# Linear attention and a two-branch FFN on one core: v of two batches cast in flight, a PSUM bank per pair, output units in halves, and a new order of work

## The chip, the cores and the metric

The kernel runs on one core of a Trainium2 chip. The metric is the device time of one execution in microseconds (us). Three runs of the kernel before gave 251.06, 251.57 and 251.97; the median is 251.57 us.

## What is computed

Eight batches of eight heads, 576 positions, 64 elements a head, go through linear attention; the result, as 4608 rows of 512, goes through a feed-forward block with two branches that are multiplied:

```python
q_p, k_p = (phi(q), phi(k))          # phi(x) = (x if x > 0 else exp(x) - 1) + 1
kv = np.einsum('bhsd,bhse->bhde', k_p, v)
z = np.sum(k_p, axis=2)
num = np.einsum('bhsd,bhde->bhse', q_p, kv)
den = np.einsum('bhsd,bhd->bhs', q_p, z)[..., None] + 1e-06
attn = num / den
x = attn.transpose(0, 2, 1, 3).reshape(4608, 512)
a = x @ w1                           # 512 x 1024
b = x @ w2
out = (a * b @ w3) @ w_out           # 1024 x 1024, 1024 x 512
```

Inputs and output are float32 in HBM; the kernel multiplies in bf16 and sums in float32.

## The kernel before

**The order is written out.** The body defines small functions ("steps") and a long string `ORDER` (L478 to L548) that lists every step with its arguments. The loop at L555 runs through it; each engine and each DMA queue gets its instructions in that order and runs them in that order, with semaphores between engines. The string is written out in the source, and nothing is moved at run time. In the names below the first number is a batch or chunk, the last letter an engine (`v` VectorE or DVE, `a` ScalarE or ACT) or a queue (`s` SyncE's or SP's, `g` GpSimd's or POOL's). `GATES` (L550) makes a few of SP's loads wait for an earlier load.

**Opening.** Since nothing is applied between w3 and w_out, the kernel multiplies them once: `l3` and `lo` load w3 and w_out by DMAs that cast to bf16, `w3t` transposes a block of w3 on TensorE (PE), `w3c` copies it, `wa` and `wf` multiply, and `wc` copies the product, `wf_sb` (L376 to L413). `lw` loads w1 and w2 with a cast (L144). `warm` steps are matmuls on zeros that keep PE busy (L113).

**Attention of a batch.** Of the 576 positions, 512 are worked on per batch and the remaining 64 of two batches together (names with `r`; they make chunk 8). `ld` loads k, q or v of a batch, 1 MB of float32, into one of five buffers (L119). phi is max(x, 0) + 1 on DVE (`t`, L172), exp on ACT (`x`, L166), and the minimum of the two on DVE (`m`, L180), which in this kernel takes two heads at a time. `v_` casts v to bf16 into the tile `vt` (L217), in which each head has 64 columns of v and one column of ones, so that one product gives kv and z. For batches 0 and 1 `kv` (L230) multiplies pairs of heads, 128x130; `kc` and `kh` (L268, L279) copy the two diagonal blocks into `kvb`. All four pairs share one tile of two PSUM banks. From batch 2 on, `kk` (L254) multiplies head by head in half-width matmuls and `kg` copies. q is transposed by PE for batches 0 and 1 (`qt`, `qc`) and by a transposing DMA on SP from batch 2 on (`qd`, L299). `na` multiplies transposed q with `kvb` for a pair (L311), `nd` divides on DVE: add, reciprocal, multiply (L317 to L319). The quotient is transposed by PE (`xp`, `xc`) for chunks 0 to 2 and by a DMA (`xd`, L363) for 3 to 7. `nar` and `ndr` are the same for the remaining positions.

**Feed-forward of a chunk.** For each of eight blocks of 128 of the 1024 columns, `f` makes a and b in two PSUM buffers with four matmuls each (L420; `fk` does a part of them), `ac` copies a to SBUF on ACT (L434), `ab` multiplies on DVE (L439). `o` makes an output block of 128 rows with eight matmuls (L445), `oc` copies it (L451), `st` stores it (L463) through POOL's queue, in the last chunks through SP's; for chunk 8 a store is two DMAs of 64 rows. `ol` (L465 to L476) is the last output unit: it goes in two halves of the columns, one copied by DVE and stored through SP's queue, one by ACT and through ACT's.

**PSUM.** Eight banks: four one-bank buffers (tag `mm`: warm, w3t, wf, qt, xp, f, o) and two two-bank buffers (tag `at`: wa, kv, kk, na, nar).

Of the kernel before, what the change touches and what calls it, by code (L numbers as in the profile page):

```python
# [18 lines left out]
def kernel(  # L19
# [71 lines left out]


    @step
    def const(i):
        if i == 0:
            nc.vector.memset(zero, 0.0)  # L96
        elif i == 1:
            make_identity(nc, ident)
        elif i == 2:
            for t in vts:  # L100
                nc.vector.memset(t[:, :, :, D:E1], 1.0)
        elif i == 3:
# [13 lines left out]
    @step  # L116
    def ld_(n, b, h0, nh, queue):
        t = got(raw, (n, b), ld, [P, H * W], F32, "ld", f"{n}32")
        return queue_of[queue].dma_start(  # L119
            out=t[:, h0 * W:(h0 + nh) * W].rearrange("p (h x) -> p h x", x=W),  # L120
            in_=src[n][b, h0:h0 + nh, 0:NJ * P, :].rearrange("h (p j) d -> p h (j d)", j=NJ))

# [53 lines left out]
    @step  # L176
    def m(n, b, h0, hp):
        d = got(ph, (n, b), phi_p, [P, KC, NJ, 2, D], BF16, n)
        s = slice((2 * hp - h0) * W, (2 * hp - h0 + 2) * W)
        nc.vector.tensor_tensor(  # L180
            out=d[:, hp].rearrange("p j u d -> p u j d"),
            in0=ts[n, b, h0][:, s].rearrange("p (u j d) -> p u j d", u=2, j=NJ),
            in1=es[n, b, h0][:, s].rearrange("p (u j d) -> p u j d", u=2, j=NJ), op=ALU.min)
# [31 lines left out]
    @step  # L215
    def v_(b, h0, nh, eng):
        copy_of[eng](  # L217
            out=vts[b % len(vts)][:, :, h0:h0 + nh, 0:D],
            in_=raw["v", b].rearrange("p (h j d) -> p j h d", h=H, j=NJ)[:, :, h0:h0 + nh])

    @step
    def vr(b, eng):
        s = b % 2
        r = slice(s * R, (s + 1) * R)
        copy_of[eng](out=vrz[r, s, :, 0:D],
                     in_=raw["vr", b // 2][r].rearrange("p (h d) -> p h d", d=D))
# [3 lines left out]
    def kv(b, hp):  # L230
        o = got(ps, ("kv", b), at_ps, [P, 2, 512], F32, "at", "kvp")
        g, a = divmod(hp, 2)
        kj = ph["k", b]
        kr = ph["kr", b // 2, 2 if b > 1 else b]
        vt = vts[b % len(vts)]
        dst = o[:, g, a * PW:(a + 1) * PW]
        for j in range(NJ):
            nc.tensor.matmul(dst, kj[:, hp, j].rearrange("p u d -> p (u d)"),
                             vt[:, j, 2 * hp:2 * hp + 2, :].rearrange("p h e -> p (h e)"),
                             start=(j == 0), stop=False)  # L240
        nc.tensor.matmul(dst, kr[:, hp * P:(hp + 1) * P],
                         vrz[:, b % 2, 2 * hp:2 * hp + 2, :].rearrange("p h e -> p (h e)"),
                         start=False, stop=True)
# [4 lines left out]
    def kk(b, hp):  # L248
        o = got(ps, ("kk", b), at_ps, [P, 2, 512], F32, "at", "kvp")[:, 0]
        kj, kr, vt = ph["k", b], ph["kr", b // 2, 2], vts[b % len(vts)]  # L250
        for j in range(NJ + 1):
            for u in range(2):
                h = 2 * hp + u
                nc.tensor.matmul(o[u * D:(u + 1) * D, hp * E1:(hp + 1) * E1],  # L254
                                 kj[:, hp, j, u] if j < NJ else kr[:, h * D:(h + 1) * D],
                                 vt[:, j, h] if j < NJ else vrz[:, b % 2, h],
                                 start=(j == 0), stop=(j == NJ))

    @step
# [48 lines left out]
    def na(b, hp):  # L308
        o = ps["na", b, hp] = at_ps.tile([P, 2, 512], F32, tag="at", name="nd")
        for j in range(NJ):  # L310
            nc.tensor.matmul(o[:, j // 2, (j % 2) * 256:(j % 2) * 256 + PW],  # L311
                             sb["qt", b][:, hp, j * P:(j + 1) * P],
                             kvb[b][:, hp].rearrange("p u e -> p (u e)"),
                             start=True, stop=True)

    def divide(o, r, dst):
        nc.vector.tensor_scalar_add(out=r, in0=o[:, :, :, D], scalar1=1e-6)  # L317
        nc.vector.reciprocal(out=r, in_=r)  # L318
        nc.vector.tensor_tensor(  # L319
            out=dst, in0=o[:, :, :, 0:D],  # L320
# [3 lines left out]
    def nd(b, hp):  # L324
        x = got(sb, ("xn", b), att, [P, NJ, DM], BF16, "xn")
        r = small.tile([P, NJ, 2], F32, tag="r4", name="r")
        o = ps["na", b, hp].rearrange("p i (a x) -> p (i a) x", a=2)[:, :, 0:PW]
        divide(o.rearrange("p j (u e) -> p j u e", e=E1), r,
               x[:, :, hp * P:(hp + 1) * P].rearrange("p j (u e) -> p j u e", u=2))

    @step
    def nar(b):
        o = ps["nar", b] = at_ps.tile([P, 2, 512], F32, tag="at", name="ndr")
        for hp in range(KC):
            g, a = divmod(hp, 2)
            nc.tensor.matmul(o[:, g, a * PW:(a + 1) * PW], sb["qtr", b // 2][:, hp, :],  # L336
                             kvb[b][:, hp].rearrange("p u e -> p (u e)"),
# [252 lines left out]
```

## Time and profile before

| what | value |
|---|---|
| median of three runs | 251.57 us |
| profiled execution: time | 251.52 us |
| profiled execution: span of the core | 249.7 us, 4327 instructions |
| PE busy | 236.0 us (95%) |
| DVE busy | 164.1 us (66%) |
| ACT busy | 122.9 us (49%) |
| chain that ended last: PE, DMA | 56%, 32% |
| DMA moved | 50.10 MB, mean 201 GB/s |
| granted TensorE clock | 1.000 |
| f (L420, chunks 0 to 7): a and b | 66.0 us each, 256 matmuls each |
| o (L445) | 62.9 us, 267 matmuls recorded |
| last matmul ends, last store lands, span ends | 246.27, 248.6, 249.7 us |

The time of an execution is some 1.8 us longer than the span between its first and last instruction. Matmuls are pipelined: the 379 ns that the page gives for one of 512 columns holds its latency, and four that follow each other start 0.86 us after the four before them. In lines of the timeline the first number is the start and the second the length in us, and the bracket at the end says how long the engine sat idle before and what ended that. A few matmul records are missing, which can look like a gap of 0.22 us.

### The profile page before, as it was taken

How to read it: one execution, taken by the hardware profiler on the slowest of the kernel's cores; microseconds unless marked ns; L12 is line 12 of the kernel's file. 1: busy time of each engine (PE TensorE's matmuls, PEld its weight loads, DVE VectorE, ACT ScalarE, POOL GpSimd, SP SyncE). 2: the span in 40 equal slices, each digit the busy share in tenths (PEclk: the TensorE clock that was granted, in tenths of full speed). 3: DMA queues.
4: the chain of work that ended last, by engine and by line, in shares of the span. 5: the costliest groups of instructions: out<-in, count | busy, mean ns of one | idle time of the engine just before them, and what ended most of it. 6: DMA issues, size and time to landing. Idle time of an engine off the chain costs nothing.

```text
span 249.7 us, 4327 instructions
## 1 busy us (share of the span) xinstructions
PE 236.0 (95%) x1620; PEld 122.9 (49%) x1636; DVE 164.1 (66%) x364; ACT 122.9 (49%) x190; POOL 36.4 (15%) x59
## 2 busy tenths in 40 slices
PE   6897889979999989999999999999999999999994
PEld 6654844445444555454444454544544444444442
DVE  7518764977868999959649889786775365042320
ACT  3409554776956774665744835153352332323211
POOL 8554720001100210011000032200001100000000
PEclk9999999999999999999999999999999999999999
DMA  6999999999998999999999699975409511210155
GB/s 120 204 265 348 214 198 294 314 248 319 336 240 227 281 294 287 211 248 351 189 265 335 182 248 260 291 175 107 105 12 128 179 22 21 91 38 29 55 144 153
DMA packets 69621, 50.10 MB, mean 201 GB/s; under 512 B 41312, under 2 KB 64096, under 8 KB 69600
## 3 DMA queue, kind: packets, MB, share of 16 engines
q1 hardware_dynamic: 60416, 31.86, 54.1%
q0 software_dynamic: 9040, 17.83, 28.0%
q8 instruction: 13, 0.21, 0.3%
q10 hardware_dynamic: 144, 0.13, 0.2%
q14 instruction: 8, 0.07, 0.1%
HBM read 38.80 MB, written 9.44 MB: 193 GB/s over the span
## 4 chain that ended last, share of the span: by engine, by line
PE 56%; DMA 32%; DVE 4%; issue 3%; ACT 2%; POOL 1%; SPq 0%; ACTq 0%; POOLq 0%; DVEq 0%
PE a_ps L420 17%; PE o_ps L445 17%; PE b_ps L420 17%; DMA v<-in_v_dram 13%; DMA q<-in_q_dram 9%; DMA w_sb<-in_moe_w_dram 4%; DMA wo<-in_moe_w_out_dram 3%; DMA k<-in_k_dram 3%; DVE xn L319 2%; PE nd L311 2%; PE kvp L254 1%; POOL w3b L159 1%; PE ndr L336 1%; PE o_ps L472 1%; ACT vt L217 1%
## 5 line engine op out<-in xcount | busy, mean ns | idle before, releaser
L420 PEld LDWEIGHTS <-w_sb 128*128 128x128 bf16 x576 | 55.6, 98 | 64.6 <-issue 0.6
L439 DVE TENSOR_TENSOR ab<-a_sb,b_ps 128x512 bf16<-128x512 f32 x72 | 49.0, 684 | 43.7 <-PE b_ps L420 40.1
L434 ACT COPY a_sb<-a_ps 128x512 f32<-128x512 f32 x72 | 42.1, 584 | 58.8 <-PE a_ps L420 52.7
L420 PE MATMUL a_ps<-xt,w_sb 128*128 128x512 bf16 x256 | 66.0, 379 | 0.5 <-ACT xt L358 0.5
L420 PE MATMUL b_ps<-xt,w_sb 128*128 128x512 bf16 x256 | 66.0, 379 | 0.0
L445 PE MATMUL o_ps<-wf_sb,ab 128*128 128x512 bf16 x267 | 62.9, 379 | 1.0 <-issue 0.2
L445 PEld LDWEIGHTS <-ab 128*128 128x128 bf16 x280 | 26.4, 98 | 30.3 <-DVE ab L439 1.2
L463 POOL DMA_DIRECT2D out_dram<-o_sb x24 | 14.5, 605 | 148.7 <-ACT o_sb L451 130.9
L451 ACT COPY o_sb<-o_ps 128x512 f32<-128x512 f32 x24 | 14.0, 585 | 34.1 <-PE o_ps L445 31.9
L319 DVE TENSOR_TENSOR xn<-nd,r 128x512 bf16<-128x512 f32 x32 | 22.1, 692 | 1.1
L166 ACT ACTIVATE e<-q 128x1024 bf16<-128x1024 f32 x16 | 16.5, 1056 | 1.8 <-DMA q<-in_q_dram 1.8
L166 ACT ACTIVATE e<-k 128x1024 bf16<-128x1024 f32 x16 | 16.4, 1058 | 0.9 <-DMA k<-in_k_dram 0.8
L451 DVE COPY o_sb<-o_ps 128x512 f32<-128x512 f32 x11 | 7.6, 687 | 8.0 <-PE o_ps L445 8.0
L217 ACT CAST vt<-v 128x1024 bf16<-128x1024 f32 (+1 forms) x11 | 10.2, 933 | 5.4 <-PE kvp L254 2.7
L180 DVE TENSOR_TENSOR k<-t,e 128x512 bf16<-128x512 bf16 x32 | 12.2, 418 | 0.4 <-ACT e L166 0.2
L172 DVE TENSOR_SCALAR t<-q 128x1024 bf16<-128x1024 f32 x16 | 10.9, 688 | 2.1 <-DMA q<-in_q_dram 2.1
L180 DVE TENSOR_TENSOR q<-t,e 128x512 bf16<-128x512 bf16 x32 | 11.9, 420 | 0.2
L311 PE MATMUL nd<-kvb,qt 128*128 128x130 bf16 x128 | 10.9, 220 | 0.9 <-DVE kvb L268 0.4
L172 DVE TENSOR_SCALAR t<-k 128x1024 bf16<-128x1024 f32 x16 | 10.5, 688 | 1.2 <-DMA k<-in_k_dram 1.1
L311 PEld LDWEIGHTS <-qt 128*128 128x128 bf16 x128 | 8.7, 98 | 4.9 <-DVE xn L319 1.0
L113 PE MATMUL warm<-zero 128*128 128x128 bf16 x116 | 9.2, 241 | 1.2 <-DVE zero L96 1.2
L318 DVE RECIPROCAL r<-r 128x8 f32<-128x8 f32 (+1 forms) x40 | 8.1, 202 | 1.4
(76 smaller groups left out, 191.6 us busy)
## 6 DMA issues: line engine op xcount, KB each, us to landing
v<-in_v_dram SPq DMA_DIRECT2D x6, 1024.0 KB, 9.8
k<-in_k_dram SPq DMA_DIRECT2D x6, 1024.0 KB, 8.7
q<-in_q_dram SPq DMA_DIRECT2D x6, 1024.0 KB, 9.2
out_dram<-o_sb POOLq DMA_DIRECT2D x24, 256.0 KB, 6.1
w3b<-in_moe_w_dram POOLq DMA_DIRECT2D x8, 256.0 KB, 8.1
out_dram<-o_sb SPq DMA_DIRECT2D x7, 256.0 KB, 2.3
v<-in_v_dram POOLq DMA_DIRECT2D x3, 512.0 KB, 18.9
out_dram<-o_sb SPq DMA_DIRECT2D x9, 128.0 KB, 2.4
```

Of the source, the lines that this page charges most:

```text
L166: return nc.scalar.activation(out=e[:, 0:nh * W], in_=raw[n, b][:, h0 * W:(h0 + nh) * W], func=AF.Exp)
L172: nc.vector.tensor_scalar(out=d[:, 0:nh * W], in0=raw[n, b][:, h0 * W:(h0 + nh) * W], scalar1=0.0, scalar2=1.0, op0=ALU.max, op1=ALU.add)
L180: nc.vector.tensor_tensor(out=d[:, hp].rearrange("p j u d -> p u j d"), in0=ts[n, b, h0][:, s].rearrange("p (u j d) -> p u j d", u=2, j=NJ ...
L217: copy_of[eng](out=vts[b % len(vts)][:, :, h0:h0 + nh, 0:D], in_=raw["v", b].rearrange("p (h j d) -> p j h d", h=H, j=NJ)[:, :, h0:h0 + nh])
L311: nc.tensor.matmul(o[:, j // 2, (j % 2) * 256:(j % 2) * 256 + PW], sb["qt", b][:, hp, j * P:(j + 1) * P], kvb[b][:, hp].rearrange("p u e - ...
L319: nc.vector.tensor_tensor(out=dst, in0=o[:, :, :, 0:D], in1=r.unsqueeze(3).to_broadcast(list(r.shape) + [D]), op=ALU.mult)
L420: nc.tensor.matmul(o, w[:, kc, f * P:(f + 1) * P], xt_of(c)[:, :, kc, :], start=(kc == 0), stop=(kc == KC - 1))
L434: return copy_of[eng](out=d, in_=ps["a", c, f])
L439: nc.vector.tensor_mul(out=d[:, f, :], in0=sb["a", c, f], in1=ps["b", c, f])
L445: nc.tensor.matmul(d, sb["ab", c][:, f, m * P:(m + 1) * P], wf_sb[:, f, :], start=(f == 0), stop=(f == FC - 1))
L451: return copy_of[eng](out=d, in_=ps["o", c, m])
L463: queue_of[queue].dma_start(out=dst, in_=sb["o", c, m][r])
```

## The change

Seven things change together.

1. `lv` loads v of batches 0 and 1 by a POOL DMA that casts to bf16, in pieces of heads as `ld` did; the casts `v:0` and `v:1` are gone.
2. `kv` reads this v directly. The column of ones isn't in it, so each of the four j gets a second matmul with a tile `ones` of two columns. A pair has a PSUM bank of its own, and two pairs share one of the two-bank tiles; `kc` and `kh` read from these.
3. The layout of a pair in `kvb`, `vt` and `vrz` is now one, 64, 64, one instead of 64, one, 64, one; the divisions and the casts of v are adapted, and `v_` takes one head of every pair at a time.
4. `m` takes four heads in one instruction, and phi's layout is position group, head, element.
5. `oh` does half of an output unit: four of the eight matmuls. Chunks 0 and 1 use it: their eight units become sixteen steps, between which other steps of PE stand.
6. `kk` is one step for four pairs, with the same matmuls in the same order; steps `kz`, `nt`, `ln` and `xm` are added to the text but not in the order; `const:12` sets `ones`, `eps` and `kvz`.
7. `ORDER` is new throughout, and `GATES` names the loads in a new sequence.

```diff
+        elif i == 12:
+            nc.vector.memset(ones, 1.0)
+            nc.vector.memset(eps, 1e-6)
+            nc.vector.memset(kvz, 0.0)
...
+    @step
+    def lv(b, h0, nh):
+        if ("vb", b) not in raw:
+            raw["vb", b] = ld.tile([P, H * W], F32, tag="ld", name="vb").bitcast(
+                BF16)[:, 0:H * W].rearrange("p (h j d) -> p h j d", h=H, j=NJ)
+        return nc.gpsimd.dma_start(
+            out=raw["vb", b][:, h0:h0 + nh].rearrange("p h j d -> p h (j d)"),
+            in_=v[b, h0:h0 + nh, 0:NJ * P, :].rearrange("h (p j) d -> p h (j d)", j=NJ))
...
-    def m(n, b, h0, hp):
+    def m(n, b, h0, nh):
+        d = got(ph, (n, b), phi_p, [P, NJ, H, D], BF16, n)
         nc.vector.tensor_tensor(
+            out=d[:, :, h0:h0 + nh].rearrange("p j h d -> p h j d"),
+            in0=ts[n, b, h0][:, 0:nh * W].rearrange("p (h j d) -> p h j d", h=nh, j=NJ),
+            in1=es[n, b, h0][:, 0:nh * W].rearrange("p (h j d) -> p h j d", h=nh, j=NJ), op=ALU.min)
...
-    def v_(b, h0, nh, eng):
+    def v_(b, u, eng):
         copy_of[eng](
+            out=of_pairs(vts[b % len(vts)])[:, :, :, 1 + u * D:1 + (u + 1) * D],
+            in_=raw["v", b].rearrange("p (c u j d) -> p u j c d", u=2, j=NJ, d=D)[:, u])
...
     def kv(b, hp):
         g, a = divmod(hp, 2)
+        dst = got(ps, ("kv", b, g), at_ps, [P, 2, 512], F32, "at", "kvp")[:, a, 0:PW]
+        kj, kr, vb = ph["k", b], ph["kr", b // 2, b], raw["vb", b]
         for j in range(NJ):
+            k2 = of_pair(kj[:, j], hp)
+            nc.tensor.matmul(dst[:, 1:PW - 1].rearrange("p (u d) -> p u d", u=2), k2,
+                             vb[:, 2 * hp:2 * hp + 2, j], start=(j == 0),
+                             stop=False, skip_group_check=True)
+            nc.tensor.matmul(dst[:, 0:PW:PW - 1], k2, ones, start=False, stop=False, skip_group_check=True)
...
+    @step
+    def oh(c, m, i):
+        o_part(c, m, range(i * FC // 2, (i + 1) * FC // 2))
```

Of the new order, the stretches that matter most, the opening from wa on, batch 1, and the end:

```text
ld:q,0,4,4,g w3t:4 lv:0,0,4 w3t:5 w3c:4,v lv:0,4,2 wf:4 warm:10,10 lv:0,6,2 l3:6 l3:7 wa:7,1
t:k,0,0,4 wc:4,a w3c:5,a lw:0,0,256 wc:3,v wc:1,a x:k,0,4,4 warm:10,11 x:q,0,0,4 wf:5 wc:5,a
m:k,0,0,4 wc:2,a vr:0,v t:k,0,4,4 m:k,0,4,4 wc:0,v lw:1,0,256 warm:10,12 kv:0,1 kv:0,0 kv:0,2
x:q,0,4,4 lw:0,1,256 t:q,0,4,4 t:q,0,0,4 warm:10,13 kh:0,2,1,a m:q,0,4,4 m:q,0,0,4 lw:1,1,256
lw:0,1,512 lw:1,1,512 kv:0,3 kc:0,0,1,a kh:0,3,1,v lr:k,1,s kh:0,2,0,a kc:0,0,0,a qt:0,2,2
kh:0,3,0,v qt:0,0,2 qc:0,0,2,v lr:v,1,s qc:0,2,2,a w3t:6 ld:k,1,0,8,g w3t:7 na:0,1 na:0,2 w3c:6,v
nd:0,1 w3c:7,a wf:6 na:0,3 xp:0,1 xc:0,1,a wc:6,a nd:0,2 ld:q,1,0,8,g nd:0,3 na:0,0 nd:0,0 wf:7
xp:0,3 wc:7,v xp:0,2 xc:0,2,v xp:0,0 xc:0,0,v const:5 xc:0,3,a f:0,1 fk:0,0,0,2 fk:0,0,2,1
...
ab:0,5 x:k,1,0,4 t:k,1,0,4 xr:k,0,1 m:k,1,0,4 f:0,4 f:0,7 mr:k,0,1 lv:1,0,4 ac:0,4,a ab:0,4 ac:0,7,a
lv:1,4,4 f:0,6 ab:0,7 x:q,1,0,4 t:q,1,0,4 vr:1,a m:q,1,0,4 f:0,2 ac:0,6,a x:q,1,4,4 kv:1,1 t:q,1,4,4
kv:1,0 ab:0,6 x:k,1,4,4 ac:0,2,a t:k,1,4,4 m:q,1,4,4 qt:1,0,2 m:k,1,4,4 ab:0,2 qt:1,2,2 ld:q,2,0,8,s
kv:1,2 oh:0,0,0 kv:1,3 qc:1,2,2,v kc:1,0,0,v kh:1,3,1,v kh:1,2,1,a kc:1,0,1,a kh:1,3,0,v kh:1,2,0,a
na:1,2 qc:1,0,2,a nd:1,2 oh:0,2,0 oh:0,2,1 na:1,0 t:q,2,4,4 oc:0,2,a ld:k,2,0,8,s xp:1,2 oh:0,0,1
const:11 oc:0,0,a xc:1,2,v x:k,2,4,4 x:q,2,4,4 na:1,1 oh:0,3,0 lp:v,1,s nd:1,0 t:k,2,4,4 nd:1,1
ld:v,2,0,8,s na:1,3 xp:1,0 oh:0,3,1 xp:1,1 oh:0,1,0 oc:0,3,a nd:1,3 xp:1,3 xc:1,0,v m:q,2,4,4
xc:1,1,a lp:k,1,s oh:0,1,1 xc:1,3,a f:1,7 m:k,2,4,4 v:2,1,v v:2,0,a oc:0,1,v x:q,2,0,4 st:0,3,g
...
m:k,2,0,4 ac:1,3,a ab:1,3 ac:1,2,a const:8 ab:1,2 ld:q,3,0,8,s qd:2 vr:2,a x:k,3,0,4 f:1,4 kk:2
...
f:1,5 ac:1,1,a x:q,3,4,4 ab:1,1 na:2,1 vr:3,v ac:1,5,a t:q,3,0,4 ab:1,5 f:1,6
...
na:4,2 ac:3,7,a t:k,5,4,4 f:3,4 t:k,5,0,4 ab:3,7 ac:3,4,a f:3,5 nd:4,2
...
f:3,3 ac:3,3,a f:4,7 m:q,5,0,4 ab:3,3 kk:5
...
ab:8,3 f:7,0 f:7,1 ac:7,0,a o:8,0 ac:7,1,a ab:7,0 o:8,3 oc:8,0,v ab:7,1 o:7,1 oc:7,1,a st:8,0,s
st:7,1,s oc:8,3,a o:7,0 o:7,2 oc:7,0,a st:7,0,s oc:7,2,v o:8,1 o:8,2 oc:8,1,a oc:8,2,a st:7,2,s
st:8,3,s ol:7,3 st:8,1,s st:8,2,s
```

On SP's queue the loads after batch 1 came as v2, k2, q2, v3, q3 before; they come as q2, k2, v2, k3, q3 now (with the small `lp` loads between, and `qd:2` after q3). `ld:v,5` stood behind `ld:k,5`, `xd:3` and `ld:q,5`; it stands directly behind `ld:k,4` now. The end before was:

```text
o:8,1 oc:8,3,a st:8,3,s o:8,0 oc:8,1,a st:8,1,s o:8,2 oc:8,0,v st:8,0,s o:7,0 oc:8,2,v st:8,2,s
oc:7,0,a st:7,0,s ol:7,3
```

## The prediction

> **What bounds the kernel now.** I read the page's forty slices first, then the busy time by stretches, TensorE's timeline, the chain of waits, and the end of the timeline by queue.
>
> ```profile
> PE   6897889979999989999999999999999999999994
> DVE  7518764977868999959649889786775365042320
> PEclk9999999999999999999999999999999999999999
> DMA  6999999999998999999999699975409511210155
> ```
>
> PE stands at 9 in all but a few slices from the tenth (about 56 us) on, at full clock, and the DMA engines are nearly full until slice 24 (150 us). So each TensorE instruction costs its whole length from there, and a load can only be early if another is late. What can be won lies where the digits fall: the opening, the stretch around 52 us, and the end. The stretches say how much (columns: stretch, length, busy us of each engine, clock, DMA share, GB/s):
>
> ```profile
> 34.40:52.00 17.60, 16.56 (x85) 7.75 (x84) 11.90 (x24) 10.53 (x15) 0.00 (x0) 1.00 1.08 274
> 52.00:64.40 12.40, 11.06 (x98) 6.79 (x97) 9.06 (x24) 9.16 (x17) 1.66 (x3) 1.00 1.13 305
> 64.40:90.00 25.60, 24.73 (x208) 12.47 (x209) 21.98 (x50) 18.88 (x30) 2.59 (x4) 1.00 1.09 264
> 160.00:215.00 55.00, 54.85 (x293) 26.50 (x293) 35.29 (x79) 20.48 (x34) 2.71 (x5) 1.00 0.45 103
> ```
>
> PE idles 1.0, 1.3, 0.9 and 0.15 us here. TensorE's timeline names the waits:
>
> ```profile
> 36.36 0.38 PE L420 MATMUL a_ps<-xt,w_sb 128*128 128x512 bf16 x1 [0.45 <-ACT xt L358]
> 51.79 0.39 PE L238 MATMUL kvp<-vt,k 128*128 128x130 bf16 x4 [0.59 <-ACT vt L217]
> 53.09 0.39 PE L238 MATMUL kvp<-vt,k 128*128 128x130 bf16 x4 [0.58 <-ACT vt L217]
> 88.70 0.40 PE L353 MATMUL xtp<-ident,xn 128*128 128x128 bf16 x4 [0.77 <-DVE xn L319]
> ```
>
> Batch 1's kv waits twice for ACT's cast of v, which waits for v itself: the chain has 19.71 us of DMA v from 32.68, then ACT vt at 52.41. From f:1,7 (64.43 us) on little idle is left: 0.77 above, 0.35 at 122.88 (another cast of v), some tenths elsewhere; about 1.8 with the unlisted ones under 0.3.
>
> **Prices.** From starts that follow each other in the timelines: a 128x512 matmul 0.216 us (f or o: 8 = 1.73), a 128x128 or 128x130 one 0.057, t 0.65 (two in 1.30), ab 0.62, a division nd 1.04 (starts 30.02, 31.07, 32.10), ACT's x 0.97, its 128x512 copies 0.55, xc on DVE 0.36.
>
> **The casts of v go (lv).** Batches 0 and 1 lose a DVE cast of 0.69 and ACT casts of 1.32 before 28 us, and ACT 1.04 and 0.63, DVE 0.43 at 50.7 to 53. In the transfer: 512 KB cast to bf16 frees TensorE at 5.89, 7.46, 8.69 and 9.89 (w3's blocks), 1.2 to 1.6 us each; 512 KB of f32 releases k's halves at 19.42 and 20.93, 1.5 each. So an lv of four heads takes -0.3 to +0.1 us against before; I take -0.15, q1 at 48.2 instead of 48.3.
>
> **A bank per pair, and the ones.** Each kv gets four matmuls of two columns. No row has that shape; the nearest are the 57 ns of 128x130 and the 16 ns of the half-width ones (40 in 0.76 us at 89.10). With 57: kv is 9 x 0.057 = 0.51 instead of 0.285; for batch 1 four times 0.23 = 0.9 us on PE (0.26 with 16 ns). Batch 0's is hidden by the wait for v. The two tiles of kv fill both `at` buffers, so na:0,1 and na:0,2 wait for all eight copies; they come after qt anyway.
>
> The Trainium skill ("TensorE: Matmul & The Clock Gate", "Back-to-back issue gap") gives about 25 ns as the floor for up to 64 columns, by which the 16 matmuls would cost 0.4 us; but its sustained 81 ns for weight load and 128 columns would make it 1.3, and the 57 of this trace speaks against that.
>
> **One minimum over four heads.** 128x1024 is shaped like t: 0.65 against 0.74 for the two (85.49, x2). Saves 0.09 x 32 = 2.8 us of DVE, off the path except where DVE is the last; costs that kv and qt start after four heads. Covered at 22 to 28 us by the wait for v, not at 52 (below).
>
> **v's destination** now starts on odd bf16 elements throughout; before, every second head did, at 0.65 to 0.69 a cast. I keep 0.65. The Trainium skill ("VectorE: DVE Perf Modes", "Mode 2×_1P") asks for 4-byte alignment for two results a cycle; if that counted, an estimate of 1024 / 0.96 GHz gives +0.5 us for each of three DVE casts, and nothing else of this sum would move.
>
> **Costed at nothing.** The new memsets (kvz at most 0.27 by zero's row, the others 0.07) lie before w3's first copy at 7.7, where DVE has only memsets. kk, na, nd, xd and qd keep their instructions, and the copies theirs by size (0.26 for 64x130). oh only splits eight matmuls; its PSUM buffer of four is held 4 to 5 us longer, which costs where qt or xp then finds none; after f:0 ends three are free, so I set 0.
>
> **Opening.** Inputs until v are the same. wa:7 stands behind w3t:4, w3t:5 and wf:4, which fills the 1.65 us that PE idled before wf at 20.77; wa ends at 21.7. DVE's queue from there: wc 0.61, m 0.65, vr 0.38, t, m 1.30, wc 0.61, t, t, m, m 2.60 = 6.15, to 28.0. kv:0,1 and kv:0,0 start at 25.3 with the first half of v, kv:0,3 ends at 27.9 (before 28.7). qt follows m:q to 28.8, qc and w3c:6 take DVE to 30.3, and four nd take it to 34.5 (before 34.26). Then wc:7, xc, xc (1.33): f:0,1 starts at 36.1. Before, at 36.36, PE had 0.86 of f behind it and wf:7 (1.73) before it; now wf:7 is done. Lead 0.26 + 1.73 - 0.86 = **1.1 us**.
>
> **Batch 1.** Eight units, 13.8: PE is at kv:1,1 at 49.9 (before 51.04). Now ACT is late, not v: from q1 at 48.2 it owes x, vr:1, ac, x, x (0.97 + 0.55 + 0.55 + 0.97 + 0.97 = 4.0), until 52.2, and DVE m:k,1,4,4 after it, 52.95. kv:1,2 53.5, oh:0,0,0 (first half of an output unit, which needs ab:0,2 at 53.6) 54.5, kv:1,3 and na:1,2 55.25. Before stood at 55.30 with those 0.86 + 0.23 undone: lead **1.1** still, the 0.9 of the ones paid. To f:1,7 there are 7.64 us of PE work: 62.9 (before 64.43), lead 1.5. But a new wait: SP now loads q2 and k2 before v2, and DVE has t:q,2,4,4 and t:k,2,4,4 ahead of nd:1,0 and nd:1,1. Behind a late k2 are queued nd:1,1, nd:1,3, xp:1,1, xp:1,3 and all of f:1. From 48.2, v1, q2 and k2 are 3.1 MB; at 274 to 305 GB/s that is 10.3 to 11.5 us: k2 at 58.5 to 59.7. DVE is there at 59.05. Loss 0 to 0.7; I take 0.4. Lead **1.1**.
>
> **Middle.** From f:1,7 both orders hold 181.0 us of PE work. The wait of 0.35 for v5 should go (ld:v,5 moves ahead of ld:k,5), but na:2,1 wants qd:2 at about 76, before f:1,6. qd:2 is issued at about 69, behind q3; before it took 6.4 us to land (71.04 to 77.48) and was wanted at 80.85. xd:4 has a margin under 1 us too (8.4 us to landing before). No row bounds the sum of such waits: below, before's 1.8 all gone; above, each transfer late by 1.5, twice. I take +0.5.
>
> **End.** Here a loss is certain in direction. Before, `ol:7,3` is last on SP:
>
> ```profile
> 238.26 7.25 SPq L463 DMA_DIRECT2D out_dram<-o_sb  x9
> 245.49 0.42 DVE L474 COPY o_sb<-o_ps 128x256 f32<-128x256 f32 x1 [1.96 <-PE o_ps L472]
> 245.94 0.34 SPq L476 DMA_DIRECT2D out_dram<-o_sb  x1
> 246.75 0.37 ACTq L476 DMA_DIRECT2D out_dram<-o_sb  x1
> ```
>
> Now st:8,1 and st:8,2 (two DMAs each) are behind it on SP, though their copies are done. ol's first half waits for DVE until 0.33 us before PE's end (246.27), so the four start from PE's end on, 0.55 apart (243.55, two in 1.10): the last at +1.7, landing 2.4 later (median 2.3, most 3.4) at +4.1. Before, ACT's half landed at 246.75 + 1.9 = 248.6, +2.35. Cost 4.1 - 2.35 = **+1.8 us** (1.4 to 2.8).
>
> **Sum.** The profiled execution took 251.52 (span 249.7), the median is 251.57. 251.5 - 1.1 + 0.5 + 1.8 = 252.7.
>
> **Rivals.**
> 1. *The loads keep up, and the order closes the gaps* (faster). k2 by 59.0 (lead 1.5), before's 1.8 of middle idle gone, end +1.6: 251.5 - 1.5 - 1.8 + 1.6 = 249.8. For: DVE is lighter by 2.8 and v5 early. Against: a DMA share of 1.05 to 1.15 to 124 us leaves no room. It decides where the middle's waits sum below 0.7.
> 2. *Loads become the bound* (slower). k2 lands as in before, 61.8 (behind a v2 that is now behind it, so unlikely whole): +2.7, and qd:2 or xd:4 1.0 late: 252.7 - 0.4 + 2.7 + 0.5 = 255.5. For: DMA full; before's HW loads took 8.7 to 9.8 us. It decides where k2 is later than 59.05, one for one.
> 3. *lv isn't cheaper*: lv at lw's pace or worse, 0.5 us per half later, delays kv:0,3 and q1: 252.7 + 1.0 = 253.7.
>
> **Numbers.** Forecast 0.5 (own range 251.4 to 254), rival 1 0.25 (249 to 250.8), rival 2 0.2 (254 to 257), rival 3 0.05. 0.3% (0.75 us) is about what a measurement tells from no change: under 250.8 only rival 1, 0.25; 250.8 to 252.3 the forecast's lower part, 0.2; above 0.55. Range 249.7 to 256.0: it leaves out the ends of rivals 1 and 2, some 0.15.
>
> **What would show it.** f:0,1 near 36.1 with wf:7 behind; kv:1,2 waiting for DVE k or ACT e, not vt; xp:1,1 waiting for DVE xn after a DVE wait for DMA k; qd:2 as releaser of na:2,1; four L463 issues on SP after L476, the span ending some 5.2 us after PE. Wrong if the span ends 3.5 us after PE, or if PE has waits over 1 us that I don't name.

## The result

The kernel after takes 251.43 us (median of 12 runs, 250.61 to 252.89), the kernel before, measured beside it, 251.33 (12 runs, 251.05 to 253.23). The ratio is 0.9991, 95% interval 0.9970 to 1.0012: no change that can be told. The forecast was 252.7, some 1.2 us slower than before; the time lies in its range, but the slowdown did not come. Ratios are of executions within 1.5% of the fastest of their kernel; only two, both of `e8_v_f32`, fall outside. The profiled execution took 250.61 us, the fastest of the twelve, with a span of 248.8; before it was 251.52 and 249.7.

The page's slices after:

```profile
PE   8899889989999999999999999999999999999991
...
DVE  2435984879889979766775697865749646333210
...
PEclk9999999999999999999999999999999999999997
DMA  6999999999987899996979959997653631300244
```

and its chain of work that ended last, by engine:

```profile
PE 88%; DMA 3%; DVE 3%; ACT 3%; issue 1%; POOL 1%; ACTq 0%; POOLq 0%
```

The chain was 56% PE and 32% DMA before; now it hardly touches a DMA. PE's last slice holds a 1, the one before a 9: work ends one slice early and something else fills the end. The stretches, cut where the stages of this kernel lie (columns as before):

```profile
36.60:52.00 15.40, 15.28 (x92) 7.57 (x92) 10.61 (x20) 9.66 (x14) 0.00 (x0) 1.00 1.10 277
52.00:63.30 11.30, 10.24 (x90) 6.00 (x90) 9.36 (x25) 6.39 (x13) 1.19 (x3) 1.00 1.16 284
63.30:90.00 26.70, 26.60 (x224) 13.53 (x223) 23.58 (x51) 18.13 (x29) 2.60 (x5) 1.00 0.89 242
160.00:215.00 55.00, 55.00 (x321) 26.43 (x320) 34.67 (x72) 22.58 (x37) 3.76 (x7) 1.00 0.54 135
```

PE idles 0.1 us in the third stretch, 0.9 before. Three marks from TensorE's timeline and the end carry the comparison (us):

| | before | after | difference |
|---|---|---|---|
| f:1,7 starts | 64.43 | 63.30 | -1.13 |
| f:1,7 to the end of PE | 181.84 | 179.95 | -1.89 |
| end of PE to the end of the span | 3.40 | 5.56 | +2.16 |
| sum: span | 249.67 | 248.81 | -0.86 |

So nothing was hidden: 3.0 us were won before PE's end and 2.2 lost behind it. The median of the kernel after is 0.8 us above its profiled execution. About half of that goes with an early opening: in eleven executions of other kernels below, with the same steps up to wa, the first wa stood at 11.70 to 12.50 us, 12.12 in the median (here 11.73). The other half is not explained here.

TensorE's timeline of the kernel after at the places that the prediction speaks of (start, length, idle before):

```profile
26.01 0.22 PE L264 MATMUL kvp<-vb,k 128*128 128x128 bf16 x1 [0.68 <-ACT wf_sb L464]
26.06 0.17 PE L267 MATMUL kvp<-ones,k 128*128 128x2 bf16 x1
26.09 0.22 PE L264 MATMUL kvp<-vb,k 128*128 128x128 bf16 x1
...
36.69 0.59 PE L471 MATMUL a_ps<-xt,w_sb 128*128 128x512 bf16 x2 [0.77 <-DVE xt L409]
...
55.37 0.39 PE L334 MATMUL nd<-kvb,qt 128*128 128x130 bf16 x4 [1.06 <-ACT kvb L303]
```

L264 is kv's product, L267 its column of ones, L334 na:1,2. The first kv waits for a copy of the weights (wc:2,a), which frees its PSUM buffer, not for v. A matmul of two columns is followed by the next one after 26 to 29 ns (27 in the mean of 32; 26.06 to 26.09 here). The end, on DVE, ACT and the two queues (L534 is ol's store, L521 the others):

```profile
242.47 0.42 DVE L532 COPY o_sb<-o_ps 128x256 f32<-128x256 f32 x1 [3.69 <-PE o_ps L530]
242.92 0.34 SPq L534 DMA_DIRECT2D out_dram<-o_sb  x1
243.33 0.37 ACT L532 COPY o_sb<-o_ps 128x256 f32<-128x256 f32 x1 [1.16 <-PE o_ps L530]
243.36 2.39 SPq L521 DMA_DIRECT2D out_dram<-o_sb  x4
243.74 0.37 ACTq L534 DMA_DIRECT2D out_dram<-o_sb  x1
```

Four issues follow ol's, 2.39 us for the four; ACT's half landed at 246.47, the last of the four at 247.76.

### The profile page after: what moved, and what is told of

Same layout as the page of the kernel before. It is cut to its first block, busy times and chain, and to the rows that moved or that the text cites. A ratio compares the mean times of both kernels' runs of the same rounds, so it can differ in the third digit from the quotient of the medians.

```text
span 248.8 us, 4329 instructions
## 1 busy us (share of the span) xinstructions
PE 238.1 (96%) x1668; PEld 125.0 (50%) x1668; DVE 159.6 (64%) x339; ACT 117.2 (47%) x183; POOL 33.9 (14%) x59
## 4 chain that ended last, share of the span: by engine, by line
PE 88%; DMA 3%; DVE 3%; ACT 3%; issue 1%; POOL 1%; ACTq 0%; POOLq 0%
PE a_ps L471 25%; PE b_ps L471 25%; PE o_ps L495 24%; DMA wo<-in_moe_w_out_dram 3%; PE nd L334 3%; PE wa L444 2%; PE kvp L282 2%; PE wf_ps L459 2%; PE kvp L264 1%; PE qtp L311 1%; ACT wf_sb L464 1%; PE ndr L387 1%; PE o_ps L530 1%; ACT e L190 1%; POOL w3b L183 1%
## 5 line engine op out<-in xcount | busy, mean ns | idle before, releaser
L495 PE MATMUL o_ps<-wf_sb,ab 128*128 128x512 bf16 x280 | 65.3, 379 | 0.0
L521 POOL DMA_DIRECT2D out_dram<-o_sb x24 | 12.9, 542 | 153.9 <-ACT o_sb L509 115.4
L509 ACT COPY o_sb<-o_ps 128x512 f32<-128x512 f32 x23 | 13.2, 586 | 30.2 <-PE o_ps L495 30.2
L509 DVE COPY o_sb<-o_ps 128x512 f32<-128x512 f32 x12 | 8.2, 686 | 14.2 <-PE o_ps L495 14.1
L334 PEld LDWEIGHTS <-qt 128*128 128x128 bf16 x128 | 9.1, 98 | 6.9 <-issue 1.6
L334 PE MATMUL nd<-kvb,qt 128*128 128x130 bf16 x128 | 11.4, 220 | 1.2 <-ACT kvb L303 1.1
L203 DVE TENSOR_TENSOR k<-t,e 128x1024 bf16<-128x1024 bf16 x16 | 10.7, 686 | 2.5 <-ACT e L190 1.2
L128 PE MATMUL warm<-zero 128*128 128x128 bf16 x116 | 10.4, 257 | 1.2 <-DVE zero L107 1.2
L203 DVE TENSOR_TENSOR q<-t,e 128x1024 bf16<-128x1024 bf16 x16 | 10.9, 683 | 0.9 <-ACT e L190 0.7
L240 ACT CAST vt<-v 128x1024 bf16<-128x1024 f32 x9 | 9.6, 1077 | 3.3 <-DMA v<-in_v_dram 3.3
L128 PEld LDWEIGHTS <-zero 128*128 128x128 bf16 x116 | 9.3, 119 | 1.9 <-DVE zero L107 1.2
```

What stands on the lines that cost most here:

```text
L128: nc.tensor.matmul(t[:, 0:P], zero[:, 0:P], zero[:, 0:P], start=True, stop=True)
L203: nc.vector.tensor_tensor(out=d[:, :, h0:h0 + nh].rearrange("p j h d -> p h j d"), in0=ts[n, b, h0][:, 0:nh * W].rearrange("p (h j d) -> p ...
L509: return copy_of[eng](out=d, in_=ps["o", c, m])
L521: queue_of[queue].dma_start(out=dst, in_=sb["o", c, m][r])
```

## The experiments

Each time stands against runs of the kernel before on the same chip. Marks are of each kernel's one profiled execution. Edits are of `ORDER` unless code is shown.

**The end, from both kernels.** `e1_end` takes the two stores out from behind ol:

```diff
-st:8,3,s ol:7,3 st:8,1,s st:8,2,s
+st:8,3,s st:8,1,s st:8,2,s ol:7,3
```

> The changed kernel with one edit in the order: the stores st:8,1 and st:8,2 stand ahead of ol:7,3 on SP instead of behind it. Theory (the changed order ends PE 3 us earlier and gives some 2 back because four DMA issues stand behind the last unit on SP): the span ends 3.4 us after PE instead of 5.6, and the time falls by 1.7 to 2.2 us, to about 249.3. Rival (the end after the last matmul is a fixed cost, or the stores' landing isn't what ends the span): no change within 0.4 us.

Measured: 250.32 us, ratio 0.9949 (0.9922 to 0.9977), tail behind PE 4.05 us. `e2_before_end` does the reverse to the kernel before: st:8,0 and st:8,2 go behind ol:7,3.

> The kernel before with its last two stores of chunk 8 (st:8,0 and st:8,2) moved behind ol:7,3 on SP. Theory: the span ends 5.4 to 5.6 us after PE instead of 3.4, and the time rises by 1.8 to 2.2 us. Rival (the end is a fixed cost): no change within 0.4 us.

Measured: 253.52 us, ratio 1.0075 (1.0045 to 1.0105), tail 5.42 in place of 3.40: 2.0 us, the size that the kernel after shows. Its end:

```profile
245.63 0.34 SPq L476 DMA_DIRECT2D out_dram<-o_sb  x1
246.02 2.40 SPq L463 DMA_DIRECT2D out_dram<-o_sb  x4
...
246.45 0.37 ACTq L476 DMA_DIRECT2D out_dram<-o_sb  x1
```

The same four in 2.40 us. In e1 0.65 was left. The stores just ahead of ol:7,3 hold SP when its half is ready (copy done at 243.5, issue at 244.03, landed at 246.35); but ACT's half landed last, at 246.82, 2.45 us after its issue, where it takes 1.87 in the kernel before. So most of the 0.65 is a slower landing beside the stores issued just before. `e9_end2` takes both away: chunk 8's units go ahead of chunk 7's, and each store stands straight behind its copy.

```diff
-o:8,0 ac:7,1,a ab:7,0 o:8,3 oc:8,0,v ab:7,1 o:7,1 oc:7,1,a st:8,0,s st:7,1,s oc:8,3,a o:7,0 o:7,2 oc:7,0,a
-st:7,0,s oc:7,2,v o:8,1 o:8,2 oc:8,1,a oc:8,2,a st:7,2,s st:8,3,s ol:7,3 st:8,1,s st:8,2,s
+o:8,0 ac:7,1,a ab:7,0 o:8,3 oc:8,0,v st:8,0,s ab:7,1 o:8,1 oc:8,3,a st:8,3,s o:8,2 oc:8,1,a st:8,1,s o:7,1
+oc:8,2,a st:8,2,s o:7,0 oc:7,1,a st:7,1,s o:7,2 oc:7,0,a st:7,0,s oc:7,2,v st:7,2,s ol:7,3
```

> The kernel after, with the last units in the order o:8,0, o:8,3, o:8,1, o:8,2, o:7,1, o:7,0, o:7,2, ol:7,3 and every store straight behind its copy, so that ol:7,3's two halves are the last on both queues. Theory 1 (the late end of the kernel after is the four issues behind ol:7,3 and nothing else): TensorE ends as in the kernel after, 180 us after f:1,7, and the span ends 3.4 us later as in the kernel before, 2.1 us less than in the kernel after (and 0.6 less than with st:8,2 just ahead of ol:7,3); ratio to the kernel before 0.990 to 0.993. Theory 2 (the last transfers share the DMA engines with the stores issued just before, so the tail is as long as these take): tail 4.5 or more, ratio 0.995 to 0.997.

Measured: 249.07 us, ratio 0.9889 (0.9849 to 0.9930); tail 3.41, f:1,7 to PE's end 179.95 as in the kernel after. Theory 1 holds for the tail; ACT's half lands 1.88 us after its issue again:

```profile
243.18 0.33 SPq L534 DMA_DIRECT2D out_dram<-o_sb  x1
243.59 0.37 ACT L532 COPY o_sb<-o_ps 128x256 f32<-128x256 f32 x1 [2.93 <-PE o_ps L530]
243.99 0.37 ACTq L534 DMA_DIRECT2D out_dram<-o_sb  x1
```

Nothing follows on SP, and the last issue is ACT's.

**The order of the loads.** `e3_v2_first` puts v of batch 2 ahead of its q and k again:

```diff
-ld:q,2,0,8,s ... ld:k,2,0,8,s ... lp:v,1,s ... ld:v,2,0,8,s
+lp:v,1,s ld:v,2,0,8,s ld:q,2,0,8,s ... ld:k,2,0,8,s
```

> The changed kernel with lp:v,1 and ld:v,2 ahead of ld:q,2 and ld:k,2 on SP, as the kernel before had it. My prediction's step (k2 later than 59.05 us costs one for one): k2 lands some 3.5 to 4.5 us later, near 61 to 62, t:k,2,4,4 waits, and f:1,7 starts 2 to 3 us later, time +2 to +3. Rival (the loss is taken back later, since the middle has slack in the loads): f:1,7 late by 2 to 3, but the time up by less than 1.

Measured: 254.65 us, ratio 1.0100 (1.0071 to 1.0129). f:1,7 at 67.36; k2 landed at 63.36, and DVE and then TensorE wait for it:

```profile
63.39 0.69 DVE L196 TENSOR_SCALAR t<-k 128x1024 bf16<-128x1024 f32 x1 [1.31 <-DMA k<-in_k_dram]
65.17 0.40 PE L404 MATMUL xtp<-ident,xn 128*128 128x128 bf16 x4 [1.33 <-DVE xn L342]
```

From f:1,7 to PE's end 180.2: the loss is kept whole. But not all of the 4.06 us at f:1,7 is the edit's. q of batch 1 landed at 50.01 (47.35 in the kernel after), before the first load that the edit moves was issued (50.80). Behind q's landing f:1,7 came at 17.35 us in place of 15.95: 1.4 us, about TensorE's wait above. So rival 2 of the prediction had the mechanism right, its price of one for one is not shown, and its condition was unmet: in the kernel after k2 landed at 57.24.

`e4_before_loads` tries in the kernel before the load order that was thought to help the middle (lp:v,2 and ld:k,3 ahead of qd:2; ld:v,5 ahead of qd:4).

> The kernel before with lp:v,2 and ld:k,3 ahead of qd:2 on SP, and ld:v,5 ahead of qd:4. Theory (before's waits in the middle, 0.9 at 88.7 and 0.5 at 122.9, came from loads that stood behind a transposing DMA that waited for DVE): both waits go, PE ends 1.2 to 1.5 us earlier, time about 250.1. Rival (the middle was gained by the lighter DVE, one minimum of four heads, or by the chunk's other order): the waits stay or move, time within 0.4 of before.

Measured: 254.31 us, ratio 1.0100 (1.0070 to 1.0129). The theory fell: the wait for v5 is gone, but k3 in front delays the transposing DMA qd:2 (landed 82.99, before 77.48), and others behind it:

```profile
83.03 0.63 PE L311 MATMUL nd<-kvb,qt 128*128 128x130 bf16 x8 [0.91 <-DMA qt<-q]
...
90.86 0.40 PE L353 MATMUL xtp<-ident,xn 128*128 128x128 bf16 x4 [0.57 <-ACT e L166]
...
116.76 1.02 PE L420 MATMUL a_ps<-xt,w_sb 128*128 128x512 bf16 x4 [0.71 <-DMA xt<-xn]
```

With the DMA engines full (share 1.16 from 68 to 90 us), one transfer early was another late. In the order of before, these moves of the loads do not take the idle out of the middle.

**The middle: minimum or half units.** `e6_m_two` undoes part 4 alone:

```diff
-        nc.vector.tensor_tensor(out=d[:, :, h0:h0 + nh]..., op=ALU.min)
+        for i in range(0, nh, 2):
+            nc.vector.tensor_tensor(out=d[:, :, h0 + i:h0 + i + 2]..., op=ALU.min)
```

> The kernel after, with the minimum again over two heads at a time (two instructions of 418 ns in place of one of 686), the order unchanged: 32 more VectorE instructions, 32 x 0.15 = 4.8 us more of VectorE time by their durations, some 2 us by the pitch at which they follow one another. Theory 1 (VectorE is off the path in the middle, the order and its loads closed the gaps there): only the opening's chain and batch 1's, with two minima each ahead of the first kv, move, by 0.1 to 0.3 us; f:1,7 to the end of TensorE stays within 0.5 us of 179.95; ratio 1.000 to 1.002. Theory 2 (the lighter VectorE is what took the idle out of the middle): f:1,7 to the end of TensorE grows by 1 to 2 us towards the 181.8 of before; ratio 1.005 to 1.009.

Measured: 251.79 us, ratio 1.0000 (0.9977 to 1.0024); f:1,7 to PE's end 180.12, 0.17 more. Theory 1. `e7_whole_o` undoes part 5 alone, each of the eight units whole at the place of its second half, as here:

```diff
-oh:1,2,0 nd:2,1 na:2,3 ab:1,6 oh:1,2,1
+nd:2,1 na:2,3 ab:1,6 o:1,2
```

> The kernel after, with the output units of chunks 0 and 1 in one step of eight matmuls each, at the place of the second half. Theory 1 (a half unit is a filler: oh:0,0,0 stands in a wait for the copies of kv:1,3 that TensorE has anyway): without it the first half's 0.86 us ahead of kv:1,3 moves behind na:1,2; kv:1,3 comes 0.86 earlier, its copies too, so na:1,2 waits as long and the sum changes by 0 to +0.5 us at f:1,7, the middle by under 0.3; ratio 0.999 to 1.002. Theory 2 (the halves let TensorE run through the stage of batch 1 and chunk 1 without idle): each of the four or five places where a half covers a wait costs 0.3 to 0.5, sum +1.5; ratio 1.005 to 1.007.

Measured: 253.38 us, ratio 1.0062 (1.0038 to 1.0086). f:1,7 to PE's end 181.42, **1.47 more**. In the kernel after TensorE's timeline reads:

```profile
78.21 0.39 PE L334 MATMUL nd<-kvb,qt 128*128 128x130 bf16 x4
78.43 1.03 PE L495 MATMUL o_ps<-wf_sb,ab 128*128 128x512 bf16 x4
79.42 0.40 PE L334 MATMUL nd<-kvb,qt 128*128 128x130 bf16 x4
```

and with whole units:

```profile
78.95 0.39 PE L334 MATMUL nd<-kvb,qt 128*128 128x130 bf16 x4
80.17 0.40 PE L334 MATMUL nd<-kvb,qt 128*128 128x130 bf16 x4 [0.83 <-DVE xn L342]
...
88.59 0.61 PE L334 MATMUL nd<-kvb,qt 128*128 128x130 bf16 x8 [0.86 <-ACT kvb L290]
```

The first wait is for a division, 1.04 us long, that empties a PSUM buffer for the next na; the second is for ACT's copy of kv of batch 3 into `kvb`. In the kernel after four matmuls, 0.86 us, stand in each of the two places (at 78.43, and at 86.12 ahead of an na that then waits 0.10). Theory 2, on the middle; ahead of f:1,7 the halves were worth 0.4 (26.61 against 27.01 us from f:0,1). Halves in the order of before, and a whole unit at the place of its first half, were not run.

**The cast of v.** `e8_v_f32` loads v of batches 0 and 1 as f32 again and casts it on DVE and ACT:

```diff
-lv:0,0,4 lv:0,4,2 lv:0,6,2 ... lv:1,0,4 lv:1,4,4
+ld:v,0,0,4,g ld:v,0,4,2,g ld:v,0,6,2,g ... ld:v,1,0,4,g ld:v,1,4,4,g
+m:k,0,4,4 v:0,1,v v:0,0,a ... v:1,1,v v:1,0,a kv:1,1
-            nc.tensor.matmul(dst[:, 1:PW - 1]..., k2, vb[:, 2 * hp:2 * hp + 2, j], ...)
-            nc.tensor.matmul(dst[:, 0:PW:PW - 1], k2, ones, ...)
+            nc.tensor.matmul(dst, k2, vt[:, j, 2 * hp:2 * hp + 2, :]..., start=(j == 0), stop=False)
```

> The kernel after, with v of batches 0 and 1 loaded as f32 and cast by VectorE and ScalarE (one cast of 128x1024 on each, ahead of that batch's first kv), and kv as five matmuls of 130 columns on the cast tile with its ones; a bank per pair stays. Theory 1 (the cast on the engines costs what their rows say, 0.69 on VectorE and 1.08 on ScalarE, beside each other, after v's landing): kv:0 starts 0.7 to 1.1 us after the 26.68 at which v has landed, so 27.6 in place of 26.01, less 0.45 us for the 16 matmuls of the ones column; f:0,1 about 1.1 us later, 37.8; batch 1 again 0.7 to 1.1 later less 0.45, f:1,7 1.3 to 1.8 us later than 63.3; ratio 1.004 to 1.007. Theory 2 (the opening is bound by other things, the at tiles and the weight copies, and batch 1 by the loads): f:1,7 within 0.5 of 63.3, ratio 0.999 to 1.002.

Measured: 255.47 us (median of four; two more took 258.92 and 260.33), ratio 1.0151 (1.0105 to 1.0196), more than either theory. The casts, on DVE and on ACT:

```profile
27.51 0.80 DVE L240 CAST vt<-v 128x1024 bf16<-128x1024 f32 x1 [1.55 <-DMA v<-in_v_dram]
27.51 1.07 ACT L240 CAST vt<-v 128x1024 bf16<-128x1024 f32 x1 [1.14 <-DMA v<-in_v_dram]
```

Both engines stand for all of v first, with everything queued behind them late as well: the first kv starts at 28.64, 2.63 later than in the kernel after (0.42 of that is a later first wa), f:0,1 at 40.14, 3.45 later, f:1,7 at 67.12, 3.8 later.

The casts alone don't explain these numbers. Behind the 2.88 us for which TensorE waited there, its granted clock fell to a half from 28.98 to 32.40 us; ten `warm` matmuls took 1.27 us at 29.93 and 0.72 at 25.03. TensorE was busy all through that stretch, so up to 1.7 us of its time are the clock's. The slices of the page show it in the fifth place, and the kernel after has no such place ahead of its last slice:

```profile
PEclk9999799999999999999999999999999999999997
...
92.45 0.63 PE L332 MATMUL nd<-kvb,qt 128*128 128x130 bf16 x8 [1.49 <-DMA qt<-q]
```

The second line is why the middle grew by 1.4 us: an na of batch 3 waits for its transposed q, which landed 7.97 us after its issue at 84.44 (4.33 in the kernel after). In all six executions the mean granted clock was 0.990 or lower, 0.981 in the two longest; in the kernel after it was 0.991 to 0.999.

The transfers differ too: 512, 256 and 256 KB of v (of float32 read) landed 1.11, 0.63 and 0.68 us after the one before with the cast in flight, 1.51, 0.73 and 0.73 without. Not all is the edit's: one block of weights (256 columns of w1 or w2) landed 2.58 us after the one before, in place of 1.3. So e8 shows that the cast in flight is worth something in this order, and not how much. In the kernel before, which has the same casts, the first kv started at 26.39 (its first wa 1.0 us earlier than here).

**What holds f:1,7.** `e5_kh_first` lets na:1,2 go ahead of the copies of kv:1,3:

```diff
-kv:1,3 qc:1,2,2,v kc:1,0,0,v kh:1,3,1,v kh:1,2,1,a kc:1,0,1,a kh:1,3,0,v kh:1,2,0,a na:1,2
+kv:1,3 qc:1,2,2,v kc:1,0,0,v kh:1,2,1,a kc:1,0,1,a kh:1,2,0,a na:1,2 kh:1,3,1,v kh:1,3,0,v
```

> The kernel after, with the two copies of kv:1,2 (kh:1,2,1,a and kh:1,2,0,a) and na:1,2 put ahead of the two DVE copies of kv:1,3. In the kernel after, na:1,2 stood 1.06 us on TensorE for a copy that ScalarE held back behind VectorE's copy of the next pair (ScalarE idle for 2.43 us). Theory 1 (that idle is on the chain up to f:1,7 and no load is due there, since k of batch 2 landed 2.1 us before its use): f:1,7 starts about 1.0 us earlier, at 62.3, and the run ends 0.8 to 1.0 us earlier, ratio 0.996 to 0.997. Theory 2 (the loads of q and k of batch 2 bound f:1,7 all the same): the wait moves to the first thing that needs a load, f:1,7 stays within 0.3 of 63.3, and the time does not move (ratio 0.999 to 1.001).

Measured: 251.06 us, ratio 0.9968 (0.9945 to 0.9991). The wait of na:1,2 shrank only from 1.06 to 0.68, as ACT's copy now waits for kv:1,3 by itself:

```profile
54.49 0.21 ACT L303 CAST kvb<-kvp 64x65 bf16<-64x65 f32 x1 [2.21 <-PE kvp L268]
...
55.13 0.39 PE L334 MATMUL nd<-kvb,qt 128*128 128x130 bf16 x4 [0.68 <-ACT kvb L303]
```

It starts when kv:1,3 ends (about 54.4), not kv:1,2 (53.2), though kv:1,3 writes the other bank of that tile. f:1,7 came at 63.07, 0.23 earlier, as theory 2 has it; PE ended at 243.38, no earlier than in the kernel after (243.25), so the trace doesn't show the 0.3% of the ratio as a gain. `e10_ident` moves const:1 ahead of l3:0.

> The kernel after, with the identity made (const:1, on GpSimd) ahead of the first issue of w3 in place of between the first and the second. In the kernel after the second block of w3 is issued at 2.46 us and w3's transposes follow its landings; in the kernel before it was issued at 2.12 and the opening's weights landed 0.35 to 0.57 us earlier (wo 11.12 against 11.69). Theory 1 (the opening is bound by its transfers one for one): the first issue of w3 0.5 us later, the second 0.35 earlier, wa:0 at 11.2 to 11.4, f:0,1 0.3 to 0.4 earlier, 36.3, and the end too; ratio 0.997 to 0.999. Theory 2 (what issues first sets the landings: the queue's total is the same, the first block later): nothing gained or lost beyond the spread of these landings from one execution to the next (wa:0 at 11.7 to 12.5), ratio 0.998 to 1.001.

Measured: 251.05 us, ratio 0.9969 (0.9947 to 0.9991), but wa at 12.02, f:0,1 at 37.06, f:1,7 at 63.63, none earlier than in the kernel after. No mark of the trace shows a gain; whether the 0.2% in the times is one stays open. `e11_open` shortens the opening on DVE:

```diff
-t:k,0,0,4 wc:4,a w3c:5,a lw:0,0,256 wc:3,v wc:1,a x:k,0,4,4 ... wc:5,a m:k,0,0,4 wc:2,a vr:0,v t:k,0,4,4
+t:k,0,0,4 m:k,0,0,4 t:k,0,4,4 wc:4,a w3c:5,a lw:0,0,256 wc:3,v wc:1,a wc:2,a x:k,0,4,4 ... vr:0,v wc:0,v
...
-m:q,0,4,4 m:q,0,0,4 ... qt:0,2,2 kh:0,3,0,v qt:0,0,2
+m:q,0,0,4 m:q,0,4,4 ... qt:0,0,2 kh:0,3,0,v qt:0,2,2
```

> The kernel after, with another order on VectorE and ScalarE in the opening: m:k,0,0,4 and t:k,0,4,4 go ahead of the copy wc:3,v, into the 2.07 us for which VectorE waits there for TensorE; wc:2,a goes ahead of x:k,0,4,4 so that kv finds its PSUM buffer free at 25.4 (in the kernel after it waited 0.68 us for that copy until 26.01); wc:5,a behind x:q,0,4,4; the minimum and the transposes of q's first half ahead of the second's. Theory 1 (VectorE bounds the opening from 22.5 us on, without idle): its chain is 1.3 us shorter, f:0,1 starts 1.0 to 1.3 us earlier, at 35.4 to 35.7; and since f:0,1 to f:1,7 took 26.4 to 27.0 us in all runs of this order, f:1,7 at 62.1 to 62.4; ratio 0.994 to 0.996. Theory 2 (batch 1 is bound by q's landing at 47.35): f:0,1 comes earlier and waits by that much more at ScalarE's x:q,1,0,4, f:1,7 moves 0.3 at most; ratio 0.998 to 1.0.

Measured: 251.70 us, ratio 0.9998 (0.9971 to 1.0025). f:0,1 starts at 36.08, yet f:1,7 at 64.45: a block of weights again landed 2.47 us after the one before, in place of 1.3, q landed 1.15 later than in the kernel after, and f:1,7 came later by the same 1.15. `e13_kq1_cast` moves that landing by loading k and q of batch 1 with the cast in flight:

```diff
-ld:k,1,0,8,g ... ld:q,1,0,8,g
+lb:k,1 ... lb:q,1        (as lv: one POOL DMA of eight heads into bf16)
```

> The kernel after, with k and q of batch 1 also loaded by GpSimd's queue with the cast to bf16 in the transfer (ScalarE's exponential and VectorE's maximum then read bf16; this rounds k and q before the exponential, a small change of the computation). In all runs of this order f:1,7 started 15.6 to 16.0 us behind the landing of q of batch 1, wherever f:0,1 stood (36.1 to 37.5), save where a batch-1 step itself was changed; these two loads take 3.17 and 2.97 us there, two lv of four heads 1.09 to 1.34 each. Theory 1 (batch 1 is bound by that landing): q lands 0.9 to 1.3 us earlier, at 46.1 to 46.4, and f:1,7 and the end come earlier by as much, f:1,7 at 62.0 to 62.4; ratio 0.993 to 0.996. Theory 2 (TensorE's own work from f:0,1 on and ScalarE's and VectorE's queues bound it, the landing only looks like it because the opening moves both): f:1,7 at 63.0 to 63.4, 16.5 to 17.2 us behind the landing; ratio 0.998 to 1.0.

Measured: 251.17 us, ratio 0.9973 (0.9950 to 0.9996). q landed at 46.94, only 0.4 earlier, and f:1,7 started at 63.25, the place that theory 2 gave. `e12_best` joins e9's end and e5's copies, `e14_best_cast` adds e11's opening and e13's loads.

> The kernel after with two repairs of its order together: the last units and stores of e9_end2, and the copies of kv:1,2 with na:1,2 ahead of those of kv:1,3 as in e5_kh_first. Each as measured alone: tail 3.41 in place of 5.56 us (-2.15), f:1,7 0.33 us earlier against q's landing (15.62 us behind it in place of 15.95). If the two add, 251.4 - 2.15 - 0.3 = 249.0, ratio to the kernel before 0.987 to 0.990. The rival, that the 0.33 is taken back between f:1,7 and the end, gives the ratio of e9_end2 alone, 0.989.

> All that gained or may gain, together: e12_best, with k and q of batch 1 cast by their transfers as in e13_kq1_cast and the opening's order of e11_open (f:0,1 0.6 us earlier). Theory 1 (batch 1 is bound by q's landing and TensorE by nothing before it): with both moved the stall at ScalarE's x:q,1,0,4 goes, f:1,7 at 61.5 to 62.0, the end 1.4 to 1.8 us ahead of e12_best, ratio 0.981 to 0.984. Theory 2 (TensorE's work from f:0,1 on bounds it): f:1,7 at 62.4 to 62.8, from f:0,1's 0.6 alone; ratio 0.985 to 0.988.

Measured: 249.01 us, ratio 0.9889 (0.9855 to 0.9924), and 248.89, 0.9872 (0.9845 to 0.9899); e9, e12 and e14 cannot be told apart. In e14 f:1,7 came at 62.81, where theory 2 had it. In e12 f:1,7 to PE's end is 180.16, 0.2 more than in e9: the little won is taken back at kk:4, which starts 0.37 us late at 103.67 (in e5 0.51), behind the landing of k of batch 4. Put side by side (us):

| run | q of batch 1 landed | f:0,1 | f:1,7 | behind q | behind f:0,1 |
|---|---|---|---|---|---|
| after | 47.35 | 36.69 | 63.30 | 15.95 | 26.61 |
| e6 | 48.12 | 37.53 | 64.12 | 16.00 | 26.59 |
| e9 | 47.54 | 36.98 | 63.55 | 16.01 | 26.57 |
| e1 | 47.98 | 36.57 | 63.92 | 15.94 | 27.35 |
| e11 | 48.50 | 36.08 | 64.45 | 15.95 | 28.37 |
| e13 | 46.94 | 36.99 | 63.25 | 16.31 | 26.26 |
| e5 | 47.45 | 36.64 | 63.07 | 15.62 | 26.43 |
| e14 | 47.12 | 36.09 | 62.81 | 15.69 | 26.72 |
| before | 48.29 | | 64.43 | 16.14 | |

In e1 and e11 f:0,1 is early and f:1,7 keeps its distance to q; in e13 q is early and f:1,7 comes no nearer to f:0,1 than 26.26. Both limits exist and lie some 0.3 us apart in the kernel after: the landing holds it, TensorE's own work (with the wait of 1.06 at na:1,2 in it) is next. TensorE's starts agree: in the kernel after it stood 0.19 and 0.14 us for DVE's q and k at 51.90 and 52.50, and e13 has neither wait. But e13 also made DVE's max shorter (last section), so it doesn't separate the landing from DVE. The two limits are why the repairs of batch 1 moved f:1,7 by only 0.05 (e13) and 0.23 us (e5).

## Why the prediction was wrong

The sum was 251.5 - 1.1 + 0.5 + 1.8. Against the profiled execution its terms stand so:

- **Lead at f:1,7: -1.1, measured -1.13.** Right in size, but by luck and not by its steps. e1 and e9 have the same order up to f:1,7 and led by 0.51 and 0.88; q of batch 1 landed at 47.35 here, and I had 48.2. f:0,1 was at 36.69, not 36.1: kv:0,1 waited for wc:2,a to free its buffer; with that mended, and DVE's order too, e11 had 36.08. The ones cost 27 ns each, 0.43 us for batch 1's sixteen, not 0.9. na:1,2 had a wait of 1.06 that I did not name. k2 landed at 57.24, not 58.5 to 59.7, and its 0.4 did not come. These cancelled because f:1,7 hung on q's landing. For lv I took 0.15 us per four heads; the runs show 0.23 to 0.28 (all of v of batch 0 landed 2.42 us after the transfer before it against 2.97 in e8, of batch 1 2.46 against 2.91).
- **End: +1.8, measured +2.16.** Right in mechanism, shown in both directions by e2 and e9; short by 0.4: the four issues took 2.39 us and not 2.2, and the last landed 4.5 us after PE's end and not 4.1.
- **Middle: +0.5, measured -1.89. This is the step that failed**, and within it the sentence "oh only splits eight matmuls ... so I set 0". I priced the halves by the work they hold, which is the same, and by the buffer they keep; not by what they fill. e7 puts them at -1.47 in this order: TensorE waited 0.83 and 0.86 us where the halves had stood. These are not the same waits as in the kernel before (0.77 for xn, 0.35 for a cast of v), so the new order and the halves belong together here. The lighter minimum is -0.17 (e6), the remaining 0.25 was not separated. The late transfers that I feared did not come: qd:2 landed at 73.48, I had put it at 76.
- **Rival 1** (the order closes the gaps, 249.8) named the right place: all of the middle's idle goes, for which it had 1.8. It named the lighter DVE and the early v5 as reasons. e6 shows that the first is not it; the early v5 takes its own wait away, 0.35 us by the profile of before, in e4, where what else was moved cost more. Rivals 2 and 3 did not occur.

With the three measured terms, 251.5 - 1.1 - 1.9 + 2.2 = 250.7, the profiled execution (250.61) is met; the median of 251.43 is not. On the casts to an odd start, the DVE cast of v took 0.69 to 0.72 us, as before. The rule in the Trainium skill ("VectorE: DVE Perf Modes", "Mode 2×_1P") that I weighed for it is not seen here; it also asks for a 16-bit type, and this cast reads float32, so these runs don't test it. For the two columns the skill's floor of about 25 ns ("TensorE: Matmul & The Clock Gate", "Back-to-back issue gap") was the better guide: 27 ns measured, where I had taken the nearest row of before, 57.

What stays open is how much of the gain ahead of f:1,7 is the cast in flight's, and what makes one block of weights land 1.2 us late in some executions.

## What to carry to other kernels

A step that splits work without changing it is worth what it fills: look in TensorE's timeline for waits of about the length of the piece (here 0.83 and 0.86 us, for a division and for a copy), before setting it to zero. Read the last store of a kernel by queue: the four issues behind the final copy on its queue cost 2.2 us here, and putting chunk 8's units ahead of the last chunk's, with each store straight behind its copy, took it back. Where an opening shows several waits, plot the stage's end against each candidate (a landing, the first matmul) over several executions; two limits 0.3 us apart made each single repair of batch 1 look useless here.

## What the runs showed of the hardware

A GpSimd DMA that casts f32 to bf16 in flight landed sooner than one that does not: the first 512 KB of v (float32 read) landed 1.07 to 1.18 us after the transfer before against 1.44 and 1.51 (e8), where the transfer before was not cast; behind another cast one, 512 KB of batch 1 took 1.31 to 1.34 (1.71 in e3) against 1.48 in e8. 1 MB of q of batch 1 took 2.70 and 2.71 against 2.81 to 3.01 in the same order (3.44 in e3). DVE's max over 128x1024 took 0.42 us from bf16 and 0.69 from f32 (e13, then the kernel after):

```profile
44.77 0.42 DVE L203 TENSOR_SCALAR t<-kb 128x1024 bf16<-128x1024 bf16 x1
```

```profile
44.47 0.69 DVE L196 TENSOR_SCALAR t<-k 128x1024 bf16<-128x1024 f32 x1
```

ACT's exponential took 1.06 from both.
